# One Pool operation per step in the jobs that build the sums of w2, in a linear-attention and SwiGLU kernel

## The chip, the cores and the metric

The kernel runs on one core of a Trainium2 chip. The metric is the time of the program on the device in microseconds (us), as the median of several executions. The engines are named as the profile names them: PE multiplies matrices (PEld loads its weights), DVE is the vector engine, ACT the activation engine, POOL the general one, and SP only issues DMAs here. SPq and POOLq are the queues of instructions with which SP and POOL issue DMAs.

## What is computed

S = 2048 tokens, D = 1024, F = 3584, 32 heads, all in float32.

```python
xn = layernorm(x)
q, k, v = split(xn @ wqkv)                      # phi(t) = t + 1 if t > 0 else exp(t), plus 1e-6
o  = phi(q) @ (phi(k)^T v) / (phi(q) . sum(phi(k)))   # per head
s  = o @ wo
g  = silu( (silu(xn @ w1) * (xn @ w3)) @ w2 )
out = x + s * g
```

## The kernel before

Every large product is done by a scheme of seven products instead of eight: operands are cut in two by two blocks (B11 to B22 of a weight, A11 to A22 of the tokens), sums of blocks are made beforehand (T1 to T4 of a weight, S1 to S4 of the tokens), and the seven products are added up by DVE. Each operand is kept as a rounded high half and a low half (`split`: ACT casts the high half, DVE subtracts to get the low one, lines 88 and 89), and `mm3` multiplies high by high, high by low and low by high (lines 96 to 98). So one of the seven products of a `gemm` is 12 matmuls of 512 columns.

The tokens are taken in two halves. In each half the seven token operands lie in SBUF in one set of tiles (`operand_tiles`), then come the keys and values (four pairs of gemms), the queries (four gemms), and 14 pairs of gemms for w1 and w3 (`hidden`), which write the hidden rows to HBM (`h_d`) and let POOL make the sums of their blocks (`four_sums`, tiles hs, lines 603 to 607). The last pair of the first half, number 13, runs its two gemms product by product side by side, and so does the first pair of the second half (keys and values). Between them SP loads the second half's token operands from HBM (`a_d`, line 564) into the same tiles, piece by piece as PE leaves each. A third phase, after both halves, does wo and w2.

w2 needs its own sums T1 to T4, and these are made during the first half by side work. Side work is a list of jobs (`jobs`) of Python generators. `gemm` calls `catch_up` after each product but the last, six times in all; each call takes one piece of `later` (the keys' transposes) or else one step of the front job, that is what lies up to its next `yield`. The instructions of the step are placed behind that product's copy and addition (`issue_after`) and, in the first half, behind the latest weight fetch. The program's order on each engine is then set by a scheduler that lays instructions out by its own estimate of time, within these limits. What is still in `jobs` at the end of a half is emitted at once (lines 593 to 595), with no such limit.

`next_work` lists the first half's jobs: four `prepare_next`, which make the second half's token operands, then 28 `weight_sums`, two for each of 14 blocks of w2 rows (u is 0 to 13, half is 0 or 1; tile w). A job of `weight_sums` loads 0.5 MB of w2 by two DMAs on SP (line 653), makes four sums of 128x256 in place on POOL (`sums_of`, lines 639 to 643) and stores 0.5 MB to `wt_d` by one DMA on SP (line 660). `go_on` loads two jobs ahead: a job's load is issued when the second job before it is done. The tiles come from a pool of three. `merge_wo`, in the second half, also calls `sums_of`, once for each of four k, on tiles of 128x512.

The rest that the steps of the prediction touch: DVE forms the weight sums of the running gemms with operations on two SBUF tiles (line 320), ACT and DVE split them (88, 89), DVE adds products from PSUM (430, 437, 443, 458, 466), and `keys_values` takes phi of the keys (472 to 474), turns them on PE (480) and multiplies them by the values (513).

Of the kernel before, what the change touches and what calls it, by code (L numbers as in the profile page):

```python
# [22 lines left out]
def tile_linear_attention_times_swiglu(  # L23
# [10 lines left out]
    nc = tc.nc  # L34
    x, out = x[0], out[0]
# [15 lines left out]
    def bank(name):  # L51
        return ps.tile([P, C], F32, tag="bank", name=name)
# [23 lines left out]
    wt_d = [dram.tile([P, 4, C], F32, name=f"wt_d{k}") for k in range(NF // 2)]  # L76
# [7 lines left out]
    def split(pair, src, bias=None):  # L84

        hi, lo = pair[:, 0], pair[:, 1]
        if bias is None:
            nc.scalar.copy(out=hi, in_=src)  # L88
            return nc.vector.tensor_sub(out=lo, in0=src, in1=hi.bitcast(F32))
        nc.scalar.activation(hi, src, AF.Identity, bias=bias)  # L90
        return nc.vector.scalar_tensor_tensor(lo, src, bias, hi.bitcast(F32), op0=ALU.add, op1=ALU.subtract)

    def mm3(acc, w, a, start, stop):

        (wh, wl), (ah, al) = w, a
        nc.tensor.matmul(acc, lhsT=wh, rhs=ah, start=start, stop=False, skip_group_check=True)  # L96
        nc.tensor.matmul(acc, lhsT=wh, rhs=al, start=False, stop=False, skip_group_check=True)  # L97
        nc.tensor.matmul(acc, lhsT=wl, rhs=ah, start=False, stop=stop, skip_group_check=True)  # L98
# [13 lines left out]
    def small(name):  # L112
        return pc.tile([P, C], F32, tag="c", name=name)
# [4 lines left out]
    def job_tile(shape, name):  # L118
        return praw.tile(shape, F32, tag="job", bufs=3, name=name)
# [516 lines left out]

    def sums_of(b11, b12, b21, b22):

        nc.gpsimd.tensor_sub(out=b11, in0=b12, in1=b11)  # L639
        nc.gpsimd.tensor_sub(out=b12, in0=b22, in1=b12)  # L640
        yield True
        nc.gpsimd.tensor_sub(out=b22, in0=b22, in1=b11)
        nc.gpsimd.tensor_sub(out=b21, in0=b21, in1=b22)

    def weight_sums(u, half):

        cols = slice(half * 2 * P, (half + 1) * 2 * P)

        def load():
            t = job_tile([P, 4, 2 * P], f"w2_{u}_{half}")  # L650
            for e in range(2):
                f = 2 * u + e
                nc.sync.dma_start(out=t[:, 2 * e:2 * e + 2],
                                  in_=w2[f * P:(f + 1) * P, :].rearrange("p (n c) -> p n c", c=C)[:, :, cols])
            return t

        def steps(t):
            yield from sums_of(*(t[:, i] for i in range(4)))
            yield True
            nc.sync.dma_start(out=wt_d[u][:, :, cols], in_=t)  # L660
            yield True

        return Job(load, steps)

# [102 lines left out]
    def merge_wo(k):  # L767

        both = []

        def load(e):
            j = k + e * (ND // 2)
            t = job_tile([P, 2, C], f"wo{j}")
            nc.sync.dma_start(out=t, in_=wo[j * P:(j + 1) * P, :].rearrange("p (n c) -> p n c", c=C))
            return t

        def steps(e, t):
            both.append(t)
            j = k + e * (ND // 2)
            f = small(f"kvf{j}")[:, :P]  # L780
            nc.vector.tensor_mul(f, hmask, kvacc[:, j])
            kvm = st.tile([P, 2, P], FR, tag="kvm", bufs=1, name=f"kvm{j}")
            split(kvm, f)
            o = []
            for n in range(2):
                o.append(pb.tile([P, 2, C], FR, tag="b", name=f"wos{j}_{n}"))
                split(o[n], t[:, n])
                yield True
            for n in range(2):
                acc = bank(f"wp{j}_{n}")  # L790
                mm3(acc, (kvm[:, 0], kvm[:, 1]), (o[n][:, 0], o[n][:, 1]), True, True)
                nc.scalar.copy(out=t[:, n], in_=acc)
                yield True
            if e:
                b = [t[:, n] for t in both for n in range(2)]
                for n, i in (("B11", 0), ("B21", 2), ("B22", 3)):
                    store(n, b[i])
                yield from sums_of(*b)
                for n, i in (("T1", 0), ("T3", 1), ("T4", 2), ("T2", 3)):
                    store(n, b[i])  # L800
                yield True

        def store(n, t):
            g, e = divmod(7 * k + PRODUCTS.index(n), 4)
            nc.sync.dma_start(out=wp_d[g][:, e], in_=t)

        return [Job(lambda e=e: load(e), lambda t, e=e: steps(e, t)) for e in range(2)]


# [184 lines left out]
    def hiddens(i, m):  # L994
        return left(m, lambda n: h_d[i][m // NT][:, PLACE[n][m % NT]], (FB[i][1] - FB[i][0]) // 2, f"B{i}")
# [7 lines left out]
    def second_weights(i, n, k):  # L1003
        if (i, n, k) not in asked:
            ask(i, n, k, small)
        return asked[i, n, k]
# [98 lines left out]
    def layer_place(n, i, k):  # L1105
# [4 lines left out]
                      lambda n, _, k, i=i: second_weights(i, n, k),  # L1110
                      lambda m, i=i: hiddens(i, m), lambda m, t, n: acc[m][:, t, n],
# [32 lines left out]
```

## Time and profile before

| | |
|---|---|
| median of 3 runs | 2382.03 us (2380.92, 2382.03, 2387.43) |
| the profiled execution, its own time | 2381.26 us |
| its span | 2379.0 us |
| PE busy | 2331.0 us, 98% of the span |
| DVE busy | 1760.0 us, 74% |
| ACT busy | 931.1 us, 39% |
| POOL busy | 716.5 us, 30% |

The span goes from the first to the last instruction of the profiled execution; the own time holds 2.26 us more around it. Times of rows are counted from the start of the span. The granted TensorE clock was 0.996 of full speed over the span. The first half ends and the second begins at about 842 us.

### The profile page before, as it was taken

What the parts mean: (1) busy time and instruction counts of PE and PEld (TensorE: products, weight loads), DVE (VectorE), ACT (ScalarE), POOL (GpSimd) and SP (SyncE); (2) the same over time, 40 slices, a digit from 0 to 9 for tenths busy, and PEclk for the clock granted to TensorE, in tenths of its full rate; (3) what the DMA queues carried; (4) which work ended last, traced back from release to release, by engine and by line L of the source; (5) the groups of instructions that cost most, each with busy time, mean ns of one, the idle gap of its engine ahead of it and who ended that gap; (6) DMA issues with size and microseconds to landing.
All of it is one profiled execution on the core that took longest, in us unless ns stands there. A gap on an engine that the chain in (4) does not pass through costs nothing.

```text
span 2379.0 us, 30872 instructions
## 1 busy us (share of the span) xinstructions
PE 2331.0 (98%) x10544; PEld 1928.3 (81%) x10544; DVE 1760.0 (74%) x2713; ACT 931.1 (39%) x1659; POOL 716.5 (30%) x880
## 2 busy tenths in 40 slices
PE   6999999999999999999999999999899999999998
PEld 5788888878888888888878888888687788888876
DVE  8755878888788675567878777887755676767798
ACT  5434554333232244445433333334323533342433
POOL 3000022449677320000344756155441000000033
PEclk9999999999999999999999999999999999999999
DMA  3211444566666661124455555456776565766688
GB/s 124 89 53 58 146 164 162 171 199 221 207 219 221 215 248 36 54 89 135 159 181 180 190 172 187 144 168 212 252 241 207 185 207 158 234 205 183 190 266 262
DMA packets 313566, 415.98 MB, mean 175 GB/s; under 512 B 21264, under 2 KB 243472, under 8 KB 313296
## 3 DMA queue, kind: packets, MB, share of 16 engines
q1 hardware_dynamic: 285568, 327.74, 43.7%
q0 software_dynamic: 27840, 86.27, 9.8%
q8 instruction: 83, 1.36, 0.2%
q14 instruction: 75, 0.61, 0.1%
HBM read 277.35 MB, written 140.25 MB: 176 GB/s over the span
## 4 chain that ended last, share of the span: by engine, by line
PE 54%; DMA 5%; DVE 3%; issue 1%; ACT 1%; POOL 0%; SPq 0%; POOLq 0%; ACTq 0%; DVEq 0%
PE cB L96 1%; PE cB L97 1%; PE dB L97 1%; PE dB L98 1%; PE cB L98 1%; PE dB L96 1%; PE aB L97 1%; PE aB L96 1%; PE aB L98 1%; DMA rA22B<-h_d 1%; DMA wpr<-wp_d 1%; DMA rS3B<-h_d 1%; PE den L724 1%; PE bB L98 1%; PE bB L97 1%
## 5 line engine op out<-in xcount | busy, mean ns | idle before, releaser
L624 POOL DMA_DIRECT2D h_d<-sg x112 | 82.8, 740 | 287.5 <-DVE sg L620 285.7
L582 POOL DMA_DIRECT2D pq_d<-pq x32 | 17.5, 547 | 478.9 <-DVE pq L474 464.9
L911 POOL DMA_DIRECT2D u_d<-uB x32 | 17.3, 541 | 406.6 <-DVE uB L894 368.4
L894 DVE TENSOR_TENSOR acc<-cB,acc 128x512 f32<-128x512 f32 x50 | 34.3, 687 | 40.6 <-PE cB L98 40.6
L894 DVE TENSOR_TENSOR acc<-dB,acc 128x512 f32<-128x512 f32 x56 | 38.5, 687 | 31.1 <-PE dB L98 30.9
L606 POOL TENSOR_TENSOR hs<-sg 128x256 f32<-128x256 f32 x56 | 59.6, 1064 | 0.0
L604 POOL TENSOR_TENSOR hs<-hs,sg 128x256 f32<-128x256 f32 x56 | 59.6, 1064 | 0.0
L603 POOL TENSOR_TENSOR qd<-qd 128x128 f32<-128x128 f32 x32 | 25.0, 781 | 113.9 <-DVE qd L756 98.8
L607 POOL TENSOR_TENSOR hs<-sg,hs 128x256 f32<-128x256 f32 x56 | 53.9, 963 | 1.2
L603 POOL TENSOR_TENSOR hs<-sg,sg 128x256 f32<-128x256 f32 x56 | 49.8, 888 | 1.1
L632 POOL DMA_DIRECT2D h_d<-hs x60 | 45.8, 765 | 4.4 <-POOL hs L607 2.7
L639 POOL TENSOR_TENSOR w<-w 128x256 f32<-128x256 f32 x28 | 29.4, 1052 | 57.1 <-DMA w<-in_B_w 53.0
L1025 POOL DMA_DIRECT2D s_d<-s x32 | 17.5, 547 | 79.9 <-DVE s L894 37.9
L88 ACT CAST XS4B<-rS4B 128x384 fp32r<-128x384 f32 (+1 forms) x40 | 19.7, 492 | 53.5 <-PE cB L98 40.9
L88 ACT CAST XA22B<-rA22B 128x384 fp32r<-128x384 f32 (+1 forms) x40 | 19.7, 492 | 48.9 <-PE aB L98 26.6
L88 ACT CAST XA11B<-rA11B 128x384 fp32r<-128x384 f32 (+1 forms) x40 | 19.7, 493 | 42.9 <-PE dB L98 24.4
L96 PE MATMUL cB<-T,XS3B 128*128 128x512 f32 x87 | 34.2, 393 | 1.6 <-ACT XS3B L88 1.6
L96 PE MATMUL aB<-B,XA11B 128*128 128x512 f32 x87 | 34.4, 396 | 1.3 <-ACT XA11B L88 1.3
L88 ACT CAST XS1B<-rS1B 128x384 fp32r<-128x384 f32 (+1 forms) x40 | 19.7, 493 | 40.6 <-PE cB L98 23.8
L513 PEld LDWEIGHTS kv<-kvr 128*128 128x128 f32 x256 | 33.5, 191 | 2.5
L96 PE MATMUL cB<-T,XA22B 128*128 128x512 f32 x87 | 34.2, 393 | 1.0 <-DVE acc L894 1.0
L88 ACT CAST XS3B<-rS3B 128x384 fp32r<-128x384 f32 (+1 forms) x40 | 19.7, 492 | 39.7 <-PE bB L98 20.4
(5847 smaller groups left out, 8723.8 us busy)
## 6 DMA issues: line engine op xcount, KB each, us to landing
h_d<-hs POOLq DMA_DIRECT2D x60, 256.0 KB, 3.3
h_d<-sg POOLq DMA_DIRECT2D x56, 256.0 KB, 3.0
w<-in_B_w SPq DMA_DIRECT2D x56, 256.0 KB
wt_d<-w SPq DMA_DIRECT2D x28, 512.0 KB
h_d<-hs SPq DMA_DIRECT2D x52, 256.0 KB
qs_d<-qd POOLq DMA_DIRECT2D x32, 384.0 KB, 4.4
pq_d<-pq POOLq DMA_DIRECT2D x32, 256.0 KB, 2.7
a_dS<-xo SPq DMA_DIRECT2D x16, 512.0 KB
```

What stands on the lines that cost most here:

```text
L88: nc.scalar.copy(out=hi, in_=src)
L96: nc.tensor.matmul(acc, lhsT=wh, rhs=ah, start=start, stop=False, skip_group_check=True)
L97: nc.tensor.matmul(acc, lhsT=wh, rhs=al, start=False, stop=False, skip_group_check=True)
L98: nc.tensor.matmul(acc, lhsT=wl, rhs=ah, start=False, stop=stop, skip_group_check=True)
L513: nc.tensor.matmul(acc, lhsT=r[:, 1, t], rhs=r[:, 0, t], start=t == 0, stop=t == C // P - 1)
L603: nc.gpsimd.tensor_add(out=s1, in0=a21, in1=a22)
L604: nc.gpsimd.tensor_sub(out=s2, in0=s1, in1=a11)
L606: nc.gpsimd.tensor_sub(out=s3, in0=a11, in1=a21)
L607: nc.gpsimd.tensor_sub(out=s4, in0=a12, in1=s2)
L624: nc.gpsimd.dma_start(out=h_d[i][2 * h + c][:, 2 * n:4 * n + 2, k], in_=src)
L632: queue.dma_start(out=h_d[i][2 * h + c][:, 6 + 4 * e:10 + 4 * e, k], in_=o[e].rearrange("p (e s) -> p e s", s=P))
L894: return V.tensor_add(out=c, in0=src, in1=c)
```

## The change

`sums_of` yields after each of its four operations, where it yielded once, after the second. `weight_sums` issues its store in the step of the fourth operation; the two yields behind the operations are gone. So a job has four steps (operation, operation, operation, operation and store) where it had three (two operations, two operations, store). `merge_wo` passes on only the second of the four yields, so that its own steps stay as they were.

```diff
--- before.py
+++ after.py
@@ -636,11 +636,9 @@
 
     def sums_of(b11, b12, b21, b22):
 
-        nc.gpsimd.tensor_sub(out=b11, in0=b12, in1=b11)
-        nc.gpsimd.tensor_sub(out=b12, in0=b22, in1=b12)
-        yield True
-        nc.gpsimd.tensor_sub(out=b22, in0=b22, in1=b11)
-        nc.gpsimd.tensor_sub(out=b21, in0=b21, in1=b22)
+        for out, a, b in ((b11, b12, b11), (b12, b22, b12), (b22, b22, b11), (b21, b21, b22)):
+            nc.gpsimd.tensor_sub(out=out, in0=a, in1=b)
+            yield True
 
     def weight_sums(u, half):
 
@@ -655,10 +653,10 @@
             return t
 
         def steps(t):
-            yield from sums_of(*(t[:, i] for i in range(4)))
-            yield True
-            nc.sync.dma_start(out=wt_d[u][:, :, cols], in_=t)
-            yield True
+            for i, _ in enumerate(sums_of(*(t[:, i] for i in range(4)))):
+                if i == 3:
+                    nc.sync.dma_start(out=wt_d[u][:, :, cols], in_=t)
+                yield True
 
         return Job(load, steps)
 
@@ -795,7 +793,9 @@
                 b = [t[:, n] for t in both for n in range(2)]
                 for n, i in (("B11", 0), ("B21", 2), ("B22", 3)):
                     store(n, b[i])
-                yield from sums_of(*b)
+                for i, _ in enumerate(sums_of(*b)):
+                    if i == 1:
+                        yield True
                 for n, i in (("T1", 0), ("T3", 1), ("T4", 2), ("T2", 3)):
                     store(n, b[i])
                 yield True
```

Lines behind the first hunk move up by two; all four operations are line 640 in the changed kernel, the load is 651, the store 658. The instructions are the same in number and form on every engine. PE's order differs in two places at the start of the second half, DVE's and ACT's from the end of pair 13 to the second pair of keys and values, and POOL's and SP's through the sums. Three places follow; where the number of a tile's buffer stands at the end of its name it carries no meaning.

**POOL, during pair 8 of the first half.** w_8_0 is the first w2 tile of block 8, hs the sums of the hidden rows, h_d their stores, L639 to L643 before and L640 now the four operations. Before:

```order
L639 TENSOR_TENSOR w_8_0_5565<-w_8_0_5565 128x256
L632 DMA h_d_1_98<-hs_8_1_1_5461 128x4x128
L632 DMA h_d_0_97<-hs_8_0_0_5492 128x4x128
L607 TENSOR_TENSOR hs_8_0_1_5493<-sg_8_10_5333,hs_8_0_0_5492 128x256
L640 TENSOR_TENSOR w_8_0_5565<-w_8_0_5565 128x256
L639 TENSOR_TENSOR w_8_1_5628<-w_8_1_5628 128x256
L632 DMA h_d_0_97<-hs_8_0_1_5493 128x4x128
L642 TENSOR_TENSOR w_8_0_5565<-w_8_0_5565 128x256
L640 TENSOR_TENSOR w_8_1_5628<-w_8_1_5628 128x256
L643 TENSOR_TENSOR w_8_0_5565<-w_8_0_5565 128x256
L642 TENSOR_TENSOR w_8_1_5628<-w_8_1_5628 128x256
L643 TENSOR_TENSOR w_8_1_5628<-w_8_1_5628 128x256
```

and now:

```order
L640 TENSOR_TENSOR w_6_0_5516<-w_6_0_5516 128x256
L632 DMA h_d_1_98<-hs_8_1_1_5434 128x4x128
L632 DMA h_d_0_97<-hs_8_0_0_5461 128x4x128
L607 TENSOR_TENSOR hs_8_0_1_5462<-sg_8_10_5308,hs_8_0_0_5461 128x256
L640 TENSOR_TENSOR w_6_0_5516<-w_6_0_5516 128x256
L640 TENSOR_TENSOR w_6_1_5596<-w_6_1_5596 128x256
L632 DMA h_d_0_97<-hs_8_0_1_5462 128x4x128
L640 TENSOR_TENSOR w_6_0_5516<-w_6_0_5516 128x256
L640 TENSOR_TENSOR w_6_1_5596<-w_6_1_5596 128x256
L640 TENSOR_TENSOR w_6_0_5516<-w_6_0_5516 128x256
L640 TENSOR_TENSOR w_6_1_5596<-w_6_1_5596 128x256 x2
L640 TENSOR_TENSOR w_7_0_5700<-w_7_0_5700 128x256 x4
```

The sums are three blocks of rows behind (6 and 7 in place of 8 and 9), and this pair holds 12 of them, all shown, in place of 16, of which the eight of w_9_0 and w_9_1 follow just behind the upper piece.

**SP, at the passage from the first half to the second.** A_1 and S_1 are the token operands of the second half, in the order in which PE uses them; wk_0, wv_0, wk_1, wv_1 the first weights of keys and values. Before:

```order
L564 DMA A_1_7019<-a_dA_162 128x2x512 x4
L564 DMA S_1_7020<-a_dS_163 128x2x512 x4
L300 DMA wk_0__6847<-in_A_wqkv 128x8x256
L564 DMA S_1_7021<-a_dS_164 128x2x512 x4
L300 DMA wv_0__6864<-in_A_wqkv 128x8x256
L564 DMA S_1_7022<-a_dS_165 128x2x512 x4
L564 DMA A_1_7023<-a_dA_166 128x2x512 x4
L564 DMA A_1_7024<-a_dA_167 128x2x512 x4
L564 DMA S_1_7025<-a_dS_168 128x2x512 x4
L300 DMA wk_1__7164<-in_A_wqkv 128x8x256
L300 DMA wv_1__7185<-in_A_wqkv 128x8x256
```

and now, from the fourth of the token operands on (S1, tile S_1_7022):

```order
L564 DMA S_1_7022<-a_dS_165 128x2x512 x4
L564 DMA A_1_7023<-a_dA_166 128x2x512 x4
L658 DMA wt_d_124<-w_12_1_6820 512x1x256
L564 DMA A_1_7024<-a_dA_167 128x2x512 x3
L651 DMA w_13_1_7006<-in_B_w 128x2x256 x2
L564 DMA A_1_7024<-a_dA_167 128x2x512
L564 DMA S_1_7025<-a_dS_168 128x2x512 x4
L658 DMA wt_d_125<-w_13_0_6904 512x1x256
L300 DMA wk_1__7164<-in_A_wqkv 128x8x256
L708 DMA pqd_0_8641<-pq_d_0_77 128x1024
L300 DMA wv_1__7185<-in_A_wqkv 128x8x256
L658 DMA wt_d_125<-w_13_1_7006 512x1x256
```

The loads and stores of the last w2 tiles now stand between the token operands, and one of the stores ahead of wk_1. Ahead of the piece shown, the loads of w_12_1 and w_13_0 and the store of w_12_0 stand between the third operand's pieces. Before, all loads and stores of w2 tiles were issued ahead of the first token operand, with three other DMAs between.

**DVE, in the second half, from the first pair of keys and values to the second.** c12v_0 adds up the last product of the first pair (dv_0), B11k_1 to T1k_1 are the weight operands of the second pair's keys, wk_1 their raw weights. Before:

```order
L89 TENSOR_TENSOR B11k_1__7187<-wk_1__7164,B11k_1__7187 128x512
L458 TENSOR_TENSOR c21k_0__7259<-ck_0__7091,uk_0__7054 128x512
L320 TENSOR_TENSOR wk_1__7164<-wk_1__7164 128x4x128 x2
L474 SCALAR_TENSOR_TENSOR pk_0_1_7261,z<-c21k_0__7259,pk_0_1_7261 128x512
L458 TENSOR_TENSOR c21v_0__7282<-cv_0__7111,uv_0__7072 128x512
L89 TENSOR_TENSOR T3k_1__7205<-wk_1__7164,T3k_1__7205 128x512
L492 SCALAR_TENSOR_TENSOR zacc<-z,zacc 128x1
L320 TENSOR_TENSOR wk_1__7164<-wk_1__7164 128x4x128
L466 TENSOR_TENSOR c12k_0__7300<-dk_0__7092,uk_0__7054 128x512
L89 TENSOR_TENSOR T2k_1__7227<-wk_1__7164,T2k_1__7227 128x512
L89 TENSOR_TENSOR T1k_1__7244<-wk_1__7164,T1k_1__7244 128x512
L320 TENSOR_TENSOR wk_1__7164<-wk_1__7164 128x4x128
```

and now:

```order
L458 TENSOR_TENSOR c21v_0__7282<-cv_0__7111,uv_0__7072 128x512
L474 SCALAR_TENSOR_TENSOR pk_0_1_7261,z<-c21k_0__7259,pk_0_1_7261 128x512
L492 SCALAR_TENSOR_TENSOR zacc<-z,zacc 128x1
L466 TENSOR_TENSOR c12k_0__7300<-dk_0__7092,uk_0__7054 128x512
L474 SCALAR_TENSOR_TENSOR pk_1_0_7302,z<-c12k_0__7300,pk_1_0_7302 128x512
L466 TENSOR_TENSOR c12v_0__7323<-dv_0__7112,uv_0__7072 128x512
L492 SCALAR_TENSOR_TENSOR zacc<-z,zacc 128x1
L89 TENSOR_TENSOR B11k_1__7187<-wk_1__7164,B11k_1__7187 128x512
L320 TENSOR_TENSOR wk_1__7164<-wk_1__7164 128x4x128 x2
L89 TENSOR_TENSOR T3k_1__7205<-wk_1__7164,T3k_1__7205 128x512
L320 TENSOR_TENSOR wk_1__7164<-wk_1__7164 128x4x128
L89 TENSOR_TENSOR T2k_1__7227<-wk_1__7164,T2k_1__7227 128x512
```

The split of B11k_1 and all that comes behind it now stand behind c12v_0. On ACT likewise the cast of B11k_1 stands behind both activations of pk_1_0 (lines 472, 473), where it stood ahead of those of pk_0_1, and the copy of uk_1 (line 414) stands ahead of the cast of T2k_1. On PE the eight transposes trk_1_1 and trv_1_1 stand behind the second matmul of ak_1, where they stood behind its twelfth.

On POOL the last nine of the 112 sums, one of w_12_1 and all of w_13_0 and w_13_1, have no product left to follow; w_12_1 and w_13_0 stand among the sums hs of pair 13 and w_13_1 behind them.

## Rows read from the trace of the kernel before

**Rows 1.** The page's first part: busy us, share of the span, instructions.
```profile
span 2379.0 us, 30872 instructions
...
PE 2331.0 (98%) x10544; PEld 1928.3 (81%) x10544; DVE 1760.0 (74%) x2713; ACT 931.1 (39%) x1659; POOL 716.5 (30%) x880
```

**Rows 2.** Waits of PE, 480 to 900 us: us in total, times, longest us.
```profile
PE cg__4270 L96 <- DVE c22g__4302 L437: 1.7, 1, 1.7
PE bk__7090 L98 <- DVE T2k__6942 L89: 0.4, 1, 0.4
```

**Rows 3.** Line 639: ns min/median/max, first and last start us; idle before it.
```profile
L639 POOL TENSOR_TENSOR w<-w x28: 727/1182/1282, 513.2 to 760.4; 128x256 f32<-128x256 f32 x28
...
  DMA w<-in_B_w: 53.0, 10
```

**Rows 4.** Stretches of 10 us: busy us by engine, PEclk, DMA share, GB/s.
```profile
720.00:730.00 10.00, 10.00 (x46) 8.29 (x45) 8.16 (x10) 1.87 (x3) 9.27 (x12) 1.00 0.34 90
730.00:740.00 10.00, 10.00 (x46) 8.29 (x45) 8.99 (x10) 2.97 (x5) 9.94 (x11) 1.00 1.04 369
...
780.00:790.00 10.00, 10.00 (x46) 8.27 (x45) 6.01 (x9) 4.26 (x8) 0.00 (x0) 1.00 0.48 168
...
860.00:870.00 10.00, 10.00 (x46) 8.28 (x45) 3.05 (x9) 4.28 (x7) 0.00 (x0) 1.00 0.74 264
```

**Rows 5.** Timeline of DVE around the passage: start us, us, line, operation, idle before.
```profile
844.60 0.68 DVE L466 TENSOR_TENSOR c12u__7004<-du__6795,uu__6755 128x512 f32<-128x512 f32 x1
845.37 0.69 DVE L620 TENSOR_TENSOR sg<-c12u__7004,sg 128x512 f32<-128x512 f32 x1
845.98 0.68 DVE L89 TENSOR_TENSOR T3v__6922<-wv__6864,T3v__6922 128x512 fp32r<-128x512 f32 x1
846.58 1.22 DVE L89 TENSOR_TENSOR T2k__6942<-wk__6847,T2k__6942 128x512 fp32r<-128x512 f32 x1
...
872.83 1.41 DVE L320 TENSOR_TENSOR wk__7164<-wk__7164 128x512 f32<-128x512 f32 x2
...
877.72 0.69 DVE L466 TENSOR_TENSOR c12k__7300<-dk__7092,uk__7054 128x512 f32<-128x512 f32 x1 [0.76 <-PE dk__7092 L98]
```

**Rows 6.** Timeline of PE there, the first matmul of a product and others: start us, us.
```profile
512.41 0.50 PE L96 MATMUL cg__4270<-A,T4g__4183 128*128 128x512 f32 x1 [1.67 <-DVE c22g__4302 L437]
...
847.86 0.50 PE L98 MATMUL bk__7090<-S,T2k__6942 128*128 128x512 f32 x1 [0.36 <-DVE T2k__6942 L89]
...
874.74 0.39 PE L96 MATMUL dk__7092<-S,B22k__7144 128*128 128x512 f32 x1
...
877.46 0.39 PE L96 MATMUL dv__7112<-S,B22v__7161 128*128 128x512 f32 x1
...
880.18 0.39 PE L96 MATMUL ak__7331<-A,B11k__7187 128*128 128x512 f32 x1
...
882.90 0.60 PE L480 MATMUL trk<-ident,pk 128*128 128x128 f32 x4
...
883.70 0.48 PE L96 MATMUL bk__7363<-S,T2k__7227 128*128 128x512 f32 x1
```

**Rows 7.** Timeline of ACT there: start us, us.
```profile
874.27 0.62 ACT L88 CAST T3k__7205<-wk__7164 128x512 fp32r<-128x512 f32 x1
...
878.56 0.63 ACT L472 ACTIVATE pk<-c12k__7300 128x512 f32<-128x512 f32 x1
879.22 0.63 ACT L473 ACTIVATE pk<-pk 128x512 f32<-128x512 f32 x1
```

**Rows 8.** Timeline of SP's DMA issues there: start us, us.
```profile
846.24 7.19 SPq L564 DMA_DIRECT2D S<-a_dS  x4
858.96 0.37 SPq L300 DMA_DIRECT2D wk__7164<-in_A_wqkv  x1
```

**Rows 9.** DMA packets in 860 to 861 and in 862 to 863 us.
```profile
DMA packets 219, 0.40 MB, mean 399 GB/s; under 512 B 12, under 2 KB 36, under 8 KB 219
...
DMA packets 357, 0.38 MB, mean 379 GB/s; under 512 B 0, under 2 KB 344, under 8 KB 357
```

## The prediction

> **What bounds the kernel now.** I read the page's first part first: PE is busy for 2331.0 of 2379.0 us, and POOL, whose instructions the change spreads, for 716.5 [rows 1]. So only what makes PE wait, or stop waiting, can move the end. The next view is PE's waits over the stretch that the change touches, 480 to 900 us: there are two, 1.7 and 0.4 us [rows 2]. The stretches of 10 us then show what lies beside PE: while w2's sums run, PE is at 10.00 of 10 and POOL at over 9, DVE between 8 and 9; after them POOL has a stretch with nothing at all; and at 860 to 870 us POOL is idle too [rows 4]. The granted clock is 1.00 in all of them [rows 4], so nothing here speaks for a change of the clock. Last I read the timelines of DVE, PE, ACT, SP and the DMAs at the passage from the first half to the second, since the order of the changed kernel differs there.
>
> **What the change takes away.** The 112 operations stay, 28 of each of four kinds of about 1.2 us [rows 3]; none is cheaper. They are off the path before: POOL waits 53.0 us in ten waits for the w2 tiles to arrive [rows 3], and nobody on PE waits for POOL [rows 2]. What spreading could give back is PE's waits in the stretch. The larger, 1.7 us, is for a DVE addition of gemm g of pair 4, and DVE's and POOL's orders are the same up to there; it ends at 512.4 us, ahead of the first sum at 513.2 [rows 3, 6]. It stays. So the most to be won is the 0.4 us of T2k at 847.86 [rows 2, 6]. **The gain is between 0 and 0.4 us; I take 0**, as T2k lies at the passage, where more work arrives than goes.
>
> **How long the sums now last.** A product takes 2.72 us (dk to dv to ak) [rows 6], a pair of gemms 14 of them, 38.1 us, with 12 steps in it. Before, 28 jobs of three steps were 84 steps, 7 pairs or 267 us by this rule; the trace has the first sum at 513.2 and the last job's first sum at 760.4 [rows 3]. Now there are 112 steps, 9.33 pairs, 356 us. From the code, the first half has 24 calls in the queries and 168 in the pairs of gemms; 5 go to the keys' transposes and 84 to prepare_next, so 103 are left and nine steps overflow. They are emitted at the half's end, and that is what the three pieces of the order show: POOL has sums of w2 until after pair 13, and SP has six loads and stores of 0.5 MB between the token operands and ahead of wk_1.
>
> **The passage, part one: until the first pair of keys and values runs.** DVE operations on two SBUF tiles take 0.68 us while POOL stands still and 1.22 us while it computes; one that reads PSUM (c12u) stays at 0.68 [rows 5]. T2k is just late before. Of the operations ahead of it the product into sg and the split T3v still went at 0.69 and 0.68 [rows 5]. If POOL's extra sums fall on both, T2k comes 2 times 0.54, or 1.1 us, later. Against that, SP now issues wv_0 ahead of two of the four pieces of the third token operand and behind one w2 tile more, 0.5 MB earlier on balance, some 1.3 us at the 399 GB/s of this stretch [rows 9]. From minus 0.4 to plus 1.1 us; **I take 0**.
>
> The Trainium skill, in "SBUF — State Buffer", section "Who interferes with whom", says more sharply that a vector instruction with two SBUF inputs and a GpSimd instruction that reads SBUF exclude one another, the later waiting for the whole of the earlier. The trace agrees in which operations suffer (c12u does not); by that rule the two operations could each lose a whole sum, 1.2 us, which would make this part plus 2.4.
>
> **Part two: the token operands.** The last of them (S4) is issued by 853.4 [rows 8], and its packets are through at about 862 us: at 860 to 861 only 36 of 219 packets are the short ones of wk_1 and wv_1, at 862 to 863 already 344 of 357 [rows 9]. PE first reads it at 874.74 (dk) [rows 6], 12.7 us later. Ahead of it there are now three loads and two stores of 0.5 MB, 2.6 MB. In the stretches of the sums a full DMA share carried 355 GB/s (369 at 1.04) or 265 (90 at 0.34) [rows 4], so this is 7.4 to 9.9 us. **S4 is in time by 3 to 5 us: cost 0.** Before, wk_1 and wv_1 were through at about 867, as a share of 0.74 in 860 to 870 says [rows 4]; one more store, 1.5 to 2 us, makes the delay 8.9 to 11.9. I estimate, from these, that wk_1, the first of the two, is there by 877.
>
> **Part three: the second pair's keys.** Here the new order binds. The cast of B11k_1 follows pk_1_0's activations, which end at 879.22 + 0.63 = 879.85 [rows 7] and can't come sooner, as they read c12k_0, which waits for PE's dk [rows 5]. With a cast at 0.62 [rows 7], the high half is there at 880.47, and PE wanted it at 880.18 [rows 6]. On DVE the low half follows pk_1_0 (taken at c12k's 0.69), c12v_0 (0.68, as c12u) and itself takes 0.68 (as T3v) [rows 5]: 879.85 + 2.05 = 881.9. PE has two matmuls (2.72 / 12 = 0.227 each) and the transposes (882.90 to 883.70, 0.80) to fill in [rows 6]: 880.47 + 0.45 + 0.80 = 881.72, so it waits 0.2 more. Ten matmuls later it is 884.2. bk needs T2k_1, and from 881.9 there follow two combinations (1.41) [rows 5], the cast of T3k (0.62) [rows 7], its low half (0.68), a combination (0.70), the cast of T2k (0.62) and its low half (0.68): 886.6. Before, bk's first matmul stood at 883.70 and its third, the first to read the low half, at 884.15. So **bk is 2.5 us late, with half a dozen handovers of some 0.05 us each 3.0**. What is late next is B21k_1, two splits and a combination behind T2k_1 (2.06 us), against ten matmuls (2.27 us) that cover it: it fits by 0.2 us. The cost is at least 2.5, unless the handovers or wk_1 add to it; if wk_1 arrives at 879.85 or later, each us more is a us more.
>
> **The rest.** PE is behind by 3 us from there, and orders after it are those of before; later waits move along with PE, so none of it comes back. merge_wo's steps are the same. **The sum: 2381.26 + 0 + 0 + 3.0 = 2384.3 us for an execution like the profiled one**, which lies 0.8 below the median; on the median 2382.03 it is **2385.0 us**. The three runs span 6.5 us, 0.27%: 0.3%, or 7.1 us, is about what can be told from no change, and my forecast lies within it.
>
> **Rivals.**
> One: POOL's sums at the passage slow both DVE operations ahead of T2k, 1.1 us on top: 2386.1 us. For it: T2k was late before [rows 6]. Against it: wv_0 comes sooner. By the rule of the Trainium skill, with 2.4 us, it would be 2387.4.
> Two: the spreading pays as far as it can and part three costs little, as DVE or ACT run ahead of what the order suggests: 2382.03 − 0.4 = 2381.6 us. For it: only 0.4 us. Against it: the order on an engine is fixed.
> Three, **slower**: the passage's DMAs. SP issues in order; a store that waits for its sum on POOL (w_12_1, behind sg_13_00; w_13_0, behind sums of pair 13) holds the token operands and wk_1 behind it. It decides once S4 is over 12.7 us late [rows 6, 9]. With 7.4 to 9.9 us of traffic and 10 us of standing still, S4 comes some 18 to 20 late, PE waits 5 to 7 us and wk_1 is as late: 2385.0 + 7 = 2392 us. For it: DMA engines are full there [rows 9]. Against it: by my count each sum is done before SP comes to its store.
> Four, **faster** by more than 7.1 us: no wait in the stretch is that long [rows 2]; only something that these views don't show.
>
> **Chances.** Forecast 0.57, one 0.15, two 0.12: these are "the same", 0.84. Three 0.13 (slower), four 0.03 (faster). The range goes from 2381.0, under rival two, to 2391.0, which takes in rival one and the lower part of three; outside lie four and the rest of three with what a median may stray, under 0.2.
>
> **What would show it.** PE in the changed profile should have its 1.7 us wait at 512 as before, none up to 842, and at the second pair's keys a wait of some 2 us for T2k_1 and under 1 us for B11k_1; line 640 should run until about 860. I am wrong if PE waits for a token operand (S4, A22) there, if wk_1 is what B11k_1 waits for, or if PE waits anywhere in pairs 5 to 13.

## The result and the profile after

The changed kernel takes **2394.69 us** in the median of five runs (2391.83 to 2399.75), against 2383.56 us for the kernel before beside it: a ratio of **1.0047, 95% interval 1.0029 to 1.0064**. It is slower by some 11 us (7 to 15), more than the 0.3% that can be told from no change, and above the top of the range that I gave. The profiled execution took 2391.83 us with a span of 2389.5.

The first part of the page of the changed kernel (as in [rows 1]) and PE's waits from 480 to 900 us (as in [rows 2]):

```profile
span 2389.5 us, 30879 instructions
...
PE 2336.4 (98%) x10544; PEld 1930.6 (81%) x10544; DVE 1770.1 (74%) x2713; ACT 931.5 (39%) x1659; POOL 715.4 (30%) x880
```

```profile
PE bk__7090 L98 <- DVE T2k__6925 L89: 2.5, 1, 2.5
PE kv L513 <- ACT kvr L481: 2.2, 1, 2.2
PE cg__4270 L96 <- DVE c22g__4302 L437: 2.1, 1, 2.1
PE bk__7363 L96 <- ACT T2k__7227 L88: 1.6, 1, 1.6
```

POOL is busy for as long as before; nothing there became dearer. Of PE's two waits before, the one at 512 us is still there (2.1 for 1.7), the one for T2k has grown from 0.4 to 2.5 us, and two are new: for the second pair's T2k, and for kvr, which no step of mine had. All three lie between 846 and 897 us. Laying PE's timelines beside each other, matmul by matmul, gives how far the changed kernel is behind:

| PE instruction | before, us | after, us | behind, us |
|---|---|---|---|
| first matmul of the product of cg that waits at 512, pair 4 | 512.41 | 512.18 | −0.2 |
| first matmul of bk, first pair | 846.88 | 846.92 | 0.0 |
| third matmul of bk (reads T2k's low half) | 847.86 | 850.14 | 2.3 |
| seventh matmul of ck, behind T2v | 854.34 | 857.01 | 2.7 |
| third matmul of ak, second pair (B11k_1's low half) | 880.63 | 884.52 | 3.9 |
| bk of the second pair, fourth matmul | 884.48 | 889.79 | 5.3 |
| kv, behind kvr | 889.25 | 896.98 | 7.7 |
| cB, near the end | 2338.89 | 2349.29 | 10.4 |

From 512 to 846.9 us, where the spread sums run, nothing is lost: one operation per product costs nothing there. In the 50 us after that 7.7 us go. The last 2.7 us come in the third phase, and it isn't shown that they are the change's: e6 below, whose time is that of the kernel before, falls behind there by 2.2 us as well (from 4.23 at 883 us to 6.45 at 2339). These are stretches of 4 us of the kernel before, of the changed kernel and of e6 around an idle time of PE (columns as in [rows 4]):

```profile
1704.00:1708.00 4.00, 3.29 (x8) 2.61 (x9) 1.33 (x4) 0.62 (x1) 0.00 (x0) 0.61 0.66 215
```

```profile
1712.00:1716.00 4.00, 3.06 (x7) 2.48 (x8) 1.55 (x4) 0.62 (x1) 0.00 (x0) 0.51 0.62 183
1716.00:1720.00 4.00, 4.00 (x13) 3.11 (x12) 2.52 (x5) 1.21 (x2) 3.04 (x6) 0.63 0.83 271
```

```profile
1708.00:1712.00 4.00, 2.19 (x5) 1.81 (x6) 1.29 (x2) 0.65 (x2) 0.00 (x0) 0.64 0.69 204
1712.00:1716.00 4.00, 4.00 (x11) 3.02 (x11) 3.18 (x5) 1.02 (x2) 1.96 (x4) 0.51 0.81 286
```

In all three the granted clock comes near its lower level (0.5, 1.2 GHz): in the changed kernel and in e6 for both stretches, in the kernel before for one (0.61), with 0.96 in the next. So the profiled execution of the kernel before spent least time there.

**The first wait, T2k.** DVE's timeline of the changed kernel ahead of it (it answers to [rows 5]), and POOL's beside it (start us, us, line, operation):

```profile
839.79 0.68 DVE L89 TENSOR_TENSOR T3k__6880<-wk__6818,T3k__6880 128x512 fp32r<-128x512 f32 x1
840.39 2.61 DVE L320 TENSOR_TENSOR wv__6839<-wv__6839 128x512 f32<-128x512 f32 x1
...
848.35 1.74 DVE L89 TENSOR_TENSOR T2k__6925<-wk__6818,T2k__6925 128x512 fp32r<-128x512 f32 x1
```

```profile
840.91 0.75 POOL L603 TENSOR_TENSOR hs<-sg,sg 128x256 f32<-128x256 f32 x1
841.61 0.74 POOL L606 TENSOR_TENSOR hs<-sg 128x256 f32<-128x256 f32 x1
842.30 1.29 POOL L640 TENSOR_TENSOR w<-w 128x256 f32<-128x256 f32 x1
```

The combination wv, on two SBUF tiles, takes 2.61 us. POOL runs two operations meanwhile at 0.75 and 0.74, its undisturbed time, and the third goes at 1.29: wv stood behind two POOL operations, not one. T2k itself takes 1.74.

**The second and third, at the second pair.** DVE, then ACT, then PE of the changed kernel (as in [rows 5], [rows 7], [rows 6]):

```profile
883.11 0.69 DVE L466 TENSOR_TENSOR c12v__7323<-dv__7112,uv__7072 128x512 f32<-128x512 f32 x1
...
883.78 0.68 DVE L89 TENSOR_TENSOR B11k__7187<-wk__7164,B11k__7187 128x512 fp32r<-128x512 f32 x1
...
888.71 0.69 DVE L89 TENSOR_TENSOR T2k__7227<-wk__7164,T2k__7227 128x512 fp32r<-128x512 f32 x1 [0.68 <-ACT T2k__7227 L88]
...
893.82 1.42 DVE L320 TENSOR_TENSOR wv__7185<-wv__7185 128x512 f32<-128x512 f32 x2
```

```profile
881.77 0.63 ACT L473 ACTIVATE pk<-pk 128x512 f32<-128x512 f32 x1
882.31 0.60 ACT L88 CAST B11k__7187<-wk__7164 128x512 fp32r<-128x512 f32 x1
...
895.33 0.62 ACT L88 CAST T3v__7347<-wv__7185 128x512 fp32r<-128x512 f32 x1 [3.03 <-DVE wv__7185 L320]
895.85 0.59 ACT L481 ACTIVATE kvr<-trk 128x512 f32<-128x512 f32 x1
```

```profile
888.73 0.50 PE L96 MATMUL bk__7363<-S,T2k__7227 128*128 128x512 f32 x1 [1.61 <-ACT T2k__7227 L88]
...
896.98 1.16 PE L513 MATMUL kv<-kvr 128*128 128x128 f32 x8 [2.24 <-ACT kvr L481]
```

The cast of B11k_1 follows pk_1_0's activation with no idle time, so it waited for its place in the order and not for wk_1's load. Its low half follows c12v_0, T2k_1's is 4.9 us behind that, and the chain goes on: the combinations of wv_1 start at 893.82, T3v_1's cast waits for them, and ACT's evacuation of the transposes, kvr, stands behind that cast. PE gets kv's operand 2.24 us late.

### The profile page after: what moved, and what is told of

Its sections match the earlier page's. It is cut to its first block, busy times and chain, and to the rows that moved or that the text cites. A ratio compares the mean times of both kernels' runs of the same rounds, so it can differ in the third digit from the quotient of the medians.

```text
span 2389.5 us, 30879 instructions
## 1 busy us (share of the span) xinstructions
PE 2336.4 (98%) x10544; PEld 1930.6 (81%) x10544; DVE 1770.1 (74%) x2713; ACT 931.5 (39%) x1659; POOL 715.4 (30%) x880
## 4 chain that ended last, share of the span: by engine, by line
PE 63%; DMA 5%; DVE 5%; issue 4%; POOL 1%; ACT 1%; SPq 0%; POOLq 0%; DVEq 0%; ACTq 0%
PE cB L96 1%; PE cB L98 1%; PE cB L97 1%; PE dB L97 1%; PE dB L98 1%; PE dB L96 1%; PE aB L98 1%; PE aB L96 1%; PE aB L97 1%; DMA wpr<-wp_d 1%; PE bB L98 1%; PE bB L97 1%; PE bB L96 1%; DMA qs_d<-qd 1%; PE kv L513 1%
## 5 line engine op out<-in xcount | busy, mean ns | idle before, releaser
L640 POOL TENSOR_TENSOR w<-w 128x256 f32<-128x256 f32 x112 | 104.0, 938 | 79.2 <-DMA w<-in_B_w 75.8
L513 PE MATMUL kv<-kvr 128*128 128x128 f32 x256 | 33.7, 275 | 2.2 <-ACT kvr L481 2.2
```

Source lines behind the costliest of these rows:

```text
L513: nc.tensor.matmul(acc, lhsT=r[:, 1, t], rhs=r[:, 0, t], start=t == 0, stop=t == C // P - 1)
L640: nc.gpsimd.tensor_sub(out=out, in0=a, in1=b)
```

## The experiments

Three theories. **A**: the loss is the passage. Its part A1: POOL's operations there hold up DVE ahead of T2k. Its part A2: the later loads and stores on SP bring another fixed order on DVE and ACT, with the second pair's splits late. **B**: one operation per product costs by itself. **C**: the token operands' transfers are late. All kernels were timed against the kernel before on the same chip.

| kernel | ratio, 95% interval | PE's wait for T2k, us | second pair's keys | kvr |
|---|---|---|---|---|
| before | 1 | 0.4 | 0 | 0 |
| changed | 1.0047 (1.0029 to 1.0064) | 2.5 | 1.6 | 2.2 |
| e8, changed again | 1.0055 (1.0037 to 1.0073) | 2.5 + 0.7 | 1.6 | 2.3 |
| e1, ends early, dense | 1.0024 (1.0015 to 1.0033) | 1.7 + 0.9 | 0 | 0 |
| e2, three steps, late | 1.0056 (1.0042 to 1.0070) | 1.5 + 1.1 | 1.6 | 2.3 |
| e3, no last sums | 1.0037 (1.0024 to 1.0050) | 0.4 | 1.5 + 1.3 | 2.2 |
| e4, sums alone | 1.0094 (1.0080 to 1.0108) | 1.9 + 0.2 | 0 | 0.3 |
| e5, rest carried on | 1.0106 (1.0087 to 1.0126) | 3.8 + 0.2 | 0 | 1.8 |
| e6, ten jobs | 1.0004 (0.9994 to 1.0015) | 0.7 | 0 | 0 |
| e7, nineteen jobs | 1.0041 (1.0025 to 1.0057) | 2.7 + 0.7 | 1.6 | 2.2 |
| e9, eight more POOL operations | 1.0022 (1.0012 to 1.0033) | 1.4, T2v 2.1 | 0 | 0.3 |
| e10, sixteen more | 1.0025 (1.0014 to 1.0037) | 4.3, T2v 0.3 | 0 | 0 |

The waits are those of one profiled execution each. A ratio also holds what the clock takes: behind the wait for T2k or T2v the granted clock fell to 0.50 to 0.56 in some stretch of 2 us in the profiles of e1, e2, e4, e5, e7, e9 and e10, and stayed at 1.00 in those of the kernel before, the changed kernel, e3, e6 and e8.

**e1.** Only jobs ahead of w_8_1 go one operation per product.

```diff
-                yield True
+                if i % 2 or 2 * u + half < 17:
+                    yield True
```

> The changed kernel, but the last eleven weight jobs (from w_8_1 on) yield only behind their second and fourth sum, so that they take two steps instead of four and all sums end before the passage; the first seventeen jobs stay at one operation per product. Theory A (the work that is left over at the end of the first half and falls on the passage): ratio to the kernel before 0.999 to 1.001, PE's wait for T2k at most 0.5 us, no wait at the second pair's B11k, T2k and kvr. Theory B (one operation per product costs by itself, wherever it is): 1.003 to 1.005, and the loss spread over pairs 5 to 13. Theory C (the token operands' transfers are late): like A here, since the loads and stores of w2 also end earlier.

The second pair's waits are gone and half the loss with them, but T2k's wait stays: a miss for A, which had at most 0.5 us there and no loss. Two steps per job were too dense. POOL runs nine sums in a row, 3.53 and 6.07 us with one DMA issue between them, and PE waits 1.7 us for DVE's c22u at 802. T2k's wait has another reason here: with SP's w2 traffic crowded ahead of it, wv_0 is late. ACT's cast of it waits until 846.58, against 838.18 before; with PE 4.3 us behind by then, the load is 4.1 us late. This kernel brought new trouble of its own and tells little.

**e2.** The kernel before, started later.

```diff
     def next_work():
 
         yield from go_on([prepare_next(i) for i in range(TH // 2)])
+        for _ in range(28):
+            yield True
         yield from go_on([weight_sums(u, half) for u in range(NF // 2) for half in range(2)])
```

> The kernel before (two operations together, three steps per job), but with 28 steps that do nothing ahead of the first weight job, so that the jobs start later and the last ones fall on the passage as in the changed kernel. A: slower, 1.003 to 1.006, with waits for T2k, and for the second pair's T2k and kvr on PE. B: 1.000, as no job goes one operation per product. C: slower too, but with PE waiting for a token operand (S4, A22) rather than for DVE and ACT.

Without a single job at one operation per product, e2 has the changed kernel's loss and its waits in the same places. B falls, as the flat stretch from 512 to 847 us had said. C falls in the form I gave it: no wait for S4 or A22.

**e3 and e4** take the change's two effects apart. e3 leaves out the last nine sums, so part of w2's sums is not computed:

```diff
-    def sums_of(b11, b12, b21, b22):
+    def sums_of(b11, b12, b21, b22, n=4):
...
-            nc.gpsimd.tensor_sub(out=out, in0=a, in1=b)
+            if i < n:
+                nc.gpsimd.tensor_sub(out=out, in0=a, in1=b)
             yield True
...
-            for i, _ in enumerate(sums_of(*(t[:, i] for i in range(4)))):
+            for i, _ in enumerate(sums_of(*(t[:, i] for i in range(4)), n={25: 3, 26: 0, 27: 0}.get(2 * u + half, 4))):
```

> The changed kernel without its last nine sums (the fourth of w_12_1, all of w_13_0 and w_13_1: this part of w2's sums is not computed); their loads, stores and steps stay, and with them the order in which the second pair's B11k stands behind c12v_0 on DVE and ACT. A1 (POOL's sums hold up DVE ahead of T2k and T2v): PE's wait for T2k falls from 2.5 us to at most 0.5, and some 2.5 us of the loss go. A2 (the order that the later loads and stores bring costs the rest): the second pair's waits, 2.6 us at the keys and 2.2 us for kvr, stay; ratio about 1.002. If instead the sums cause all of it: 0.999 to 1.001 and no wait there. B: 1.003 to 1.005. C: the loss stays whole, 1.003 to 1.005, with waits for transfers.

e4 leaves out the loads and stores there, and runs the last three jobs later:

```diff
-    def weight_sums(u, half):
+    kept = []
+
+    def weight_sums(u, half, stand_in=False):
...
+            if stand_in and kept:
+                return kept[0]
...
+            if stand_in:
+                kept.append(t)
...
-                if i == 3:
+                if i == 3 and not (stand_in and (u, half) != (12, 0)):
...
-        yield from go_on([weight_sums(u, half) for u in range(NF // 2) for half in range(2)])
+        yield from go_on([weight_sums(u, half, 2 * u + half > 23) for u in range(NF // 2) for half in range(2)])
...
+        work += [weight_sums(12, 1), weight_sums(13, 0), weight_sums(13, 1)]
```

> The changed kernel, but at the passage the sums of the last three jobs run on the tile of w_12_0, without loads and stores of their own; the three true jobs run in the second half. POOL's work at the passage stays, SP's six loads and stores leave it. A1: PE's wait for T2k stays, 1.5 to 2.5 us. A2: the second pair's waits shrink, from 4.8 us to 0 to 1.5 us in all, as B11k stands earlier on DVE; ratio 1.001 to 1.002. B: 1.003 to 1.005. C: 1.000, as there is nothing left that makes the transfers late.

PE's waits of e3, then of e4, from 480 to 900 us:

```profile
PE kv L513 <- ACT kvr L481: 2.2, 1, 2.2
...
PE ak__7322 L96 <- ACT B11k__7178 L88: 1.5, 1, 1.5
PE bk__7354 L96 <- ACT T2k__7218 L88: 1.3, 1, 1.3
PE bk__7081 L98 <- DVE T2k__6925 L89: 0.4, 1, 0.4
```

```profile
PE bk__7078 L98 <- DVE T2k__6919 L89: 1.9, 1, 1.9
...
PE kv L513 <- ACT kvr L481: 0.3, 1, 0.3
```

Without the sums T2k's wait is back at 0.4; the second pair's waits stay. Without the loads and stores T2k's wait stays at 1.9, and the second pair's are gone but for 0.3 us. A1 and A2 are two causes with two places. One thing more lies in e4's wait for T2k: wv_0's cast stands at 843.75, 2.1 us late with PE 3.5 us behind. In e6 below it is as late, without w2's sums at the passage, and T2k's wait is 0.7, so most of e4's wait is left to the sums. e3's ratio is above what I wrote (1.0037 for 1.002): its order differs from the changed kernel's in one more thing. PE takes dk and dv of the first pair in turns, so dk ends later, and c12k_0 and B11k_1 behind it:

```profile
880.68 0.69 DVE L466 TENSOR_TENSOR c12k__7291<-dk__7083,uk__7045 128x512 f32<-128x512 f32 x1 [3.48 <-PE dk__7083 L98]
```

e4's total is no measure of the passage: its three jobs collide with later work, PE waits 18.5 us for ACT's XA11s, and of the 31 us by which its profile is behind in the end, 23 are lost beyond 900 us.

**e5.** What is left over goes on in the second half.

```diff
+        if h:
+            jobs.extend(left_over)
...
-        for j, _ in jobs:
-            run(j)
+        if h:
+            for j, _ in jobs:
+                run(j)
+        else:
+            left_over.extend(jobs)
         jobs.clear()
+
+    left_over = []
```

> The changed kernel, but the nine steps that are left at the end of the first half are not emitted there; they go on beside the second half's queries. Sums of w_12_1 and w_13_0 still run on POOL at the passage, w_13_1 does not, and B11k of the second pair stands ahead of c12k_0 and pk_1_0 on DVE and ACT. A1 (POOL's sums hold up DVE ahead of T2k): PE's wait for T2k stays, 1.5 to 2.5 us. A2 (order on DVE and ACT): the second pair's waits for keys, 2.6 us in the changed kernel, fall to 0 to 1 us, that for kvr from 2.2 to at most 1; ratio 1.001 to 1.003. B (one operation per product costs by itself): unchanged, 1.003 to 1.006.

At the passage as A has it for the keys: T2k's wait stays (3.8), theirs are gone, and that for kvr is 1.8, more than the 1 that I allowed. Over all it is worse by 1%: the leftover work delays the second half's jobs, and PE waits 9.1 us for XA11s and 7.4 us for a c22u of the second half's hidden block. Putting the work off has a price too.

**e6 and e7**, the dose: one operation per product for the first 10 or 19 of 28 jobs, three steps as before for the rest. The diff of e6; e7 has 19 for 10.

```diff
                 if i == 3:
+                    if 2 * u + half >= 10:
+                        yield True
                     nc.sync.dma_start(out=wt_d[u][:, :, cols], in_=t)
-                yield True
+                if i % 2 or 2 * u + half < 10:
+                    yield True
```

> The changed kernel with one operation per product in the first ten weight jobs only; the other eighteen go in three steps as before, so that all 94 steps fit into the 103 that are there. DVE's and ACT's order at the passage is that of before, and POOL's last sum ends ahead of it. A: ratio 0.999 to 1.001, no wait of PE over 0.5 us from 513 us to 900. B: 10/28 of the loss, 1.0015 to 1.002, spread over pairs 5 to 8.

> The same with the first nineteen jobs, 103 steps, which is just what fits: no step is left over, but w_13_1's four sums, its load and the last three stores stand at the passage, and B11k of the second pair stands behind pk_1_0 and c12v_0 on DVE and ACT as in the changed kernel. A1: with four sums in place of nine the wait for T2k is between 0.4 and 1.5 us. A2: the second pair's waits, 4.8 us for keys and kvr, stay though nothing is left over; ratio 1.002 to 1.003. If what is left over is the cause as such: 0.999 to 1.001. B: 1.003.

Lines of POOL's sums in the changed kernel and in e6 (first and last start, as in [rows 3], which has one of the four kinds):

```profile
L640 POOL TENSOR_TENSOR w<-w x112: 724/836/1290, 512.9 to 867.2; 128x256 f32<-128x256 f32 x112
```

```profile
L640 POOL TENSOR_TENSOR w<-w x112: 723/960/1265, 515.0 to 804.1; 128x256 f32<-128x256 f32 x112
```

e6's sums end at 804, ahead of the passage, and its time is that of the kernel before to 0.15%. Its wait for T2k, 0.7 us, is a little above the 0.5 that I allowed. e7 separates two things that I had taken for one: nothing is left over, and yet the loss is whole. Its last load and three stores of w2 stand among the token operands, and the order on DVE and ACT is the changed kernel's. So what counts is not that steps overflow but that w2's traffic reaches into the passage. T2k's wait is above what A1 allowed, and the ratio above the 1.003 that I wrote. Part of the wait comes from wv_0's load, which I had not thought of; ACT's row of e7:

```profile
844.26 0.62 ACT L88 CAST B11v__6876<-wv__6851 128x512 fp32r<-128x512 f32 x1 [5.57 <-DMA wv__6851<-in_A_wqkv]
```

Before, this cast stood at 838.18; with PE 2.6 us behind it is 3.5 us late. In the changed kernel it isn't: 837.92.

**e8**, the changed kernel unaltered.

> The changed kernel once more, beside the other three on the same chip: 1.003 to 1.006, PE's waits for T2k (2.5 us), for the second pair's T2k (1.6) and for kvr (2.2) in the same places to 0.3 us if the order fixes them, elsewhere or of other length if chance does.

The same waits in the same places; only T2k's is 0.7 us longer, more than the 0.3 that I allowed, as it splits into 2.5 for its high half and 0.7 for its low one. The DVE operation that makes it late is the surprise of this study. DVE's row, and POOL's rows beside it:

```profile
845.21 5.00 DVE L320 TENSOR_TENSOR wv__6839<-wv__6839 128x512 f32<-128x512 f32 x1
```

```profile
845.73 0.74 POOL L603 TENSOR_TENSOR hs<-sg,sg 128x256 f32<-128x256 f32 x1
846.42 0.74 POOL L606 TENSOR_TENSOR hs<-sg 128x256 f32<-128x256 f32 x1
847.12 0.74 POOL L640 TENSOR_TENSOR w<-w 128x256 f32<-128x256 f32 x1
847.81 0.73 POOL L604 TENSOR_TENSOR hs<-hs,sg 128x256 f32<-128x256 f32 x1
848.50 0.73 POOL L640 TENSOR_TENSOR w<-w 128x256 f32<-128x256 f32 x1
849.19 0.77 POOL L632 DMA_DIRECT2D h_d<-hs  x1
```

The operation that takes 0.68 alone stood behind five POOL operations in a row, each at its undisturbed 0.73 to 0.74. (e5 has the same: 5.02 us for wv_0's combination.) It need not have been a surprise. In the kernel before, thirteen DVE operations on two SBUF tiles take 2.1 to 3.2 us, five of them beside w2's sums between 592 and 745 us (2.26 to 2.62). This is the longest, DVE's row and then POOL's beside it:

```profile
1509.38 3.18 DVE L89 TENSOR_TENSOR B22g__12411<-wg__12112,B22g__12411 128x512 fp32r<-128x512 f32 x1 [0.31 <-ACT B22g__12411 L88]
```

```profile
1509.19 0.74 POOL L603 TENSOR_TENSOR hs<-sg,sg 128x256 f32<-128x256 f32 x1
1509.88 0.74 POOL L606 TENSOR_TENSOR hs<-sg 128x256 f32<-128x256 f32 x1
1510.58 0.73 POOL L607 TENSOR_TENSOR hs<-sg,hs 128x256 f32<-128x256 f32 x1
1511.27 0.74 POOL L604 TENSOR_TENSOR hs<-hs,sg 128x256 f32<-128x256 f32 x1
```

None of them makes PE wait between 480 and 900 us, so they don't show in [rows 2].

**e9 and e10** add POOL operations to the kernel before and nothing else, to test that. The diff is that of e9, where `kept` holds w2's tiles and its last is w_13_1; e10 has `range(4)`, over the tile's four parts.

```diff
             for e, _ in enumerate(four_sums(sg[0, c], sg[1, c], *o)):
+                if h == 0 and pair == NF // 2 - 1:
+                    for q in range(2):
+                        nc.gpsimd.tensor_sub(out=kept[-1][:, 2 * e + q], in0=o[e][:, :2 * P], in1=kept[-1][:, 2 * e + q])
```

> The kernel before, with eight more POOL operations of a sum's size at the passage: behind the hidden block's sums of the first half's last pair, on w_13_1's tile, which has been stored by then. No load or store is added, and DVE's and ACT's order ahead of the second pair is that of before. A1 (POOL's operations in a row hold up DVE's operations on two SBUF tiles): DVE operations of 2 to 5 us among wv, wk, T3v and T2k of the first pair, PE's wait for T2k 1.5 to 4.5 us instead of 0.4, no wait at the second pair's keys and kvr above 0.5; ratio 1.000 to 1.002. If the place of loads and stores were the cause of that wait too: the wait for T2k stays at 0.4 us, ratio 1.000.

> The same with sixteen more POOL operations. A1 with whole runs of POOL operations ahead of one of DVE's: the longest DVE operation grows with the run, to 4 to 9 us, the wait for T2k is 4 to 10 us; ratio 1.001 to 1.004. If one DVE operation waits for one POOL operation at most: none above 2.6 us and the wait for T2k as with eight.

DVE's longest operations of e9, POOL's rows beside the second of them, and DVE's longest of e10:

```profile
850.93 1.90 DVE L89 TENSOR_TENSOR T2k__6942<-wk__6847,T2k__6942 128x512 fp32r<-128x512 f32 x1
...
855.04 4.31 DVE L89 TENSOR_TENSOR T2v__6974<-wv__6864,T2v__6974 128x512 fp32r<-128x512 f32 x1
```

```profile
855.31 0.75 POOL L604 TENSOR_TENSOR hs<-hs,sg 128x256 f32<-128x256 f32 x1
856.01 2.79 POOL L633 TENSOR_TENSOR w<-hs,w 128x256 f32<-128x256 f32 x4
```

```profile
851.01 4.04 DVE L89 TENSOR_TENSOR T3v__6922<-wv__6864,T3v__6922 128x512 fp32r<-128x512 f32 x1
...
858.38 4.78 DVE L89 TENSOR_TENSOR T2v__6978<-wv__6864,T2v__6978 128x512 fp32r<-128x512 f32 x1
```

Eight POOL operations cost 1.0022, the clock's part included, with no load or store added and the second pair's keys in time: A1 is shown by itself. T2v is held as T2k is, and in e9 it costs PE more (2.1 against 1.4, a little under what I wrote for T2k). Twice as many operations don't double it: between them DVE also gets in at 1.2 us each, and the longest is 4.78, behind five of them.

## Why the prediction was wrong

- **The gain, 0**: right. The wait at 512 us stayed, T2k's was not won back.
- **How long the sums last**: right in the count, nine steps, and 7 us short in time, as POOL's last sum starts at 867.2, not "about 860". But e7 shows that the overflow as such was the wrong thing to count.
- **Part one failed, by its size.** I took 0, with 1.1 us as the most, from "T2k comes 2 times 0.54, or 1.1 us, later": every DVE operation loses at most the difference of 1.22 and 0.68. The operations lost up to 1.93 us in the changed kernel (2.61 − 0.68) and 4.32 in e8 (5.00 − 0.68), and the kernel before has one that lost 2.50 (3.18 − 0.68). I also left wv out of the sum, since it stood at 1.22 us already (841.18 on DVE's timeline before, ahead of the rows in [rows 5]), as if it could lose no more. From the kernel before to the changed one, wv went from 1.22 to 2.61, sg from 0.69 to 1.21, T3v from 0.68 to 0.91 and T2k from 1.22 to 1.74. PE was 2.3 us late at T2k and 2.7 at T2v. wv_0's earlier place on SP gave 0.26 us at most (837.92 for 838.18, with PE itself 0.2 earlier), not 1.3. And c12u of [rows 5], which was to show that an operation that reads PSUM is not slowed, ran while POOL computed nothing; c12g of the kernel before shows it (0.68 at 839.98, with POOL computing from 839.41 to 840.66).
- Rival one had this mechanism, at half its price. By the Trainium skill's "SBUF — State Buffer", section "Who interferes with whom", where two operations lose a whole sum each, I had 2.4 for the part, and PE lost 2.3. The agreement is in the size only. The section has the later instruction wait for the one that holds the ports; in e8 one DVE instruction waits for five, so the wait measured there is longer than one instruction's.
- **Part two, the token operands, 0**: right. PE waits for none of them.
- **Part three, the second pair's keys, 3.0**: right in place, chain and size. PE goes from 2.7 to 5.3 us behind, 2.6. (My own terms, 2.5 and six handovers of 0.05, make 2.8.) e3 and e4 show that it comes with the order, and so with w2's loads and stores, and not with the sums.
- **The rest failed.** "orders after it are those of before; later waits move along with PE, so none of it comes back". They don't: kvr came 2.4 us later still (5.3 to 7.7). I followed DVE's chain to T2k_1 and B21k_1 and stopped there, where it "fits by 0.2 us". But before, T3v_1's cast stood at 885.38 and PE came to kv only at 889.25, and the chain had grown later by 9.95 us (895.33) while PE was 5.3 behind. The slack was used up. The term was 0, and it measured 2.4.

So 2.7 + 2.6 + 2.4 = 7.7 us where I had 0 + 3.0 + 0. What is left of the 11 us lies within the interval and within what single profiled executions differ by.

- **Rival three** had the sign and the wrong cause: no wait for S4, A22 or wk_1 in any run. A transfer does matter in e1, e2 and e7, where wv_0 is 2 to 4 us late (it is 2 us late in e4 and e6 too), but not in the changed kernel.

None of the three signs that I had named for being wrong came: PE waited for no token operand, B11k_1 not for wk_1, and PE nowhere in pairs 5 to 13. All three looked at other places than the two terms that failed.

Open: by what rule the fixed order puts B11k_1 behind c12v_0 when w2's traffic stands nearer to wk_1 on SP; the runs show only that the two go together. The changed kernel, e2, e3, e7 and e8 have the late order, and a store of w2 on SP between the fourth token operand and wk_1 (between 846 and 868 us); the kernel before, e1, e4, e5, e6, e9 and e10 have neither. No version beat the kernel before; the waits that it has left at the passage are 0.4 us.

## What to carry to other kernels

When steps are spread thinner, look first at the end of the stretch that must hold them: here the spreading was free for 330 us, and the 7.7 us that can be traced to it were lost where its tail ran into the next phase. Price a DVE operation beside POOL by the whole row of POOL operations that may run ahead of it, not by one of them, and price each operation of the chain, also those that are already slowed; the trace of the kernel before may hold the long ones already, so look at the longest operations of their kind over the whole span and not only at those near the change. And where an order has changed, follow the chain on each engine until it has its old lead again, not only to the first operation that is late.

## What the hardware showed that I had not expected

- A DVE operation on two SBUF tiles can stay behind four or five POOL operations in a row: 5.00 us in e8, 5.02 in e5, 4.31 in e9, 4.78 in e10, for 0.68 alone. At other times DVE and POOL alternate at about 1.2 us each, and POOL is then slowed as well (0.74 to 1.2). e8 and the changed kernel are the same program, and the same operation took 5.00 and 2.61. What decides it no run shows.
- A wait of 2 to 3 us on PE does or does not bring the clock down. Stretches of 5 us behind T2k's wait, of the changed kernel and of e2:

```profile
855.00:860.00 5.00, 5.00 (x24) 4.14 (x23) 5.00 (x8) 1.27 (x3) 2.50 (x3) 1.00 1.05 404
```

```profile
855.00:860.00 5.00, 5.00 (x15) 3.91 (x14) 5.00 (x5) 3.11 (x6) 4.98 (x6) 0.58 1.04 406
```

In e2 the granted clock is near its lower level for most of it, and the same 5 us hold 15 matmuls instead of 24. The wait was 2.5 us in one piece in the changed kernel and 1.5 + 1.1 in e2. But e8, with 2.5 + 0.7, kept 1.00, and e9, with 2.1 in one piece at T2v, fell to 0.50 from 860 to 862 us; so neither the length nor the number of pieces decides it here. The price is of the size of the waits: in e7 and e8 PE waits 7.2 and 7.0 us at the passage, and over it, from 846 to 900 us of the kernel before, e7 falls 12.7 us further behind, with the clock down twice, and e8 8.3.
